# One batch's value loads ahead of GpSimd's gate, and two batches' strided scores one and two tiles later

## The chip, the cores and the metric

The kernel runs on one core of one Trainium2 chip. A core has TensorE (PE in the profile: matmuls; PEld are its weight loads), VectorE (DVE), ScalarE (ACT), GpSimd (POOL) and SyncE (SP), and 16 DMA engines that serve the transfers which these engines issue. The metric is the device time of one execution in microseconds (us). The kernel before was run three times: 310.98, 311.5 and 312.55 us, median 311.5 us. The profile is of one more execution.

## The reference

Windowed attention, then a two-layer network, in float32. Eight batches, eight heads, 576 positions, head dimension 64:

```python
scores = scale * np.matmul(q, k.transpose(0, 1, 3, 2))
rel = pos[:, None] - pos[None, :]
mask_plain = (rel >= 0) & (rel < window)                                   # window = 32
mask_dil = (rel >= 0) & (rel < window * dilation) & (rel % dilation == 0)  # dilation = 4
masks = np.stack([mask_plain if h < H // 2 else mask_dil for h in range(H)], axis=0)
scores = np.where(masks[None], scores, -1e9)
attn = softmax(scores)             # with 1e-9 added to the sum
attn_out = np.matmul(attn, v)
x = attn_out.transpose(0, 2, 1, 3).reshape(B * S, H * D)   # 4608 tokens of 512
h = x @ w_in                                               # 512 x 2048
out = (h * sigmoid(h)) @ w_out                             # 2048 x 512
```

Heads 0 to 3 are "plain" (each query sees the 32 positions up to its own), heads 4 to 7 are "strided" (32 positions in steps of 4).

## The kernel before, in words

**Two kinds of work in one stream.** The order of all instructions is written out by hand. The frame is the network: for each batch b, `layer1(b, f)` (lines 712 to 727) makes 16 tiles of the first layer, f = 0 to 15. A tile is 8 matmuls into `h`, and ScalarE's Silu from `h` into `gT`. `layer2` (lines 769 to 791) then makes four output tiles `o` for an even batch and five for an odd one, each of 16 matmuls in four groups of four, which VectorE copies and SyncE stores. Between the tiles stands the attention of the batches that follow. `plan_of(b)` (lines 811 to 929) is a timetable: `at(s, fn, ...)` puts a call at step s of batch b, and `plan(s)` makes the calls of step s in the order in which they were put there. Steps 0 to 15 stand ahead of the tiles f = 0 to 15, step 16 ahead of the first group of layer 2, step 17 ahead of the second group, and so on.

**Attention of one batch.** z = 0 means the plain heads and z = 1 the strided ones.
- `load_qk` or `load_rows` (123 to 144) bring queries and keys into one of two `nat` buffers. GpSimd issues them, and they convert float32 to float16 on the way. `load_rows(b)` of batch 3 and 4 starts with a memset.
- From batch 3 on, `cross(b, z)` (146 to 159) has SyncE issue DMA transposes into `plain` (L152, two of them) or `strided` (L158, L159). Batch 1 and 2 use TensorE for it (`transpose`).
- `scores(b, z)` (491 to 531): 64 small matmuls into `s` and 16 (strided) or 8 (plain) into `ss`, at L391 or L379; then VectorE's masking and maxima (L512, L521, L528). `shift` (L538) subtracts the maxima, for one half of the heads.
- `exps`, `normal`: exponentials on ScalarE, sums and normalization on VectorE; `turn_by_dma` transposes the result by a DMA that SyncE issues.
- `load_v(b)` (173 to 193) brings the values into `vw`, of which there are two, used in turn: two transfers of L177, two of L185, one of L190, all issued by GpSimd. Part of the values is wanted a second time at other partitions: `shift_plain`, `shift_class` (L205) and `shift_over` (L210) copy it, on VectorE or, as `shift_v`, by DMAs that SyncE issues.
- `values(b, z)` (604 to 631): 64 matmuls into `x` (L627) and 8 or 16 into `xs` (L691), which `finish` copies to `xT`, the first layer's input.

**What stands around the change.** During batch 1, step 2 has SyncE issue the shifts of batch 2's values and the transposes of batch 3 (`cross(3, 0)` and `cross(3, 1)`). Step 17 gives GpSimd, in this order: a copy of one column of `plain` into a tile called `latch` (line 876; the profile files it under L927, where the timetable makes its calls), which can run only when the plain transposes of batch 3 have landed and so holds back everything that GpSimd issues after it; then `load_v(3)`; then `load_rows(4)`. Step 21 has the plain scores of batch 3, step 28 the transposes of batch 4. During batch 2, step 0 gives GpSimd `load_v(4)` and `load_rows(5)`; step 6 has the plain values of batch 3, step 11 its strided scores with `shift`, step 12 `cross(5, 0)`, `shift_class(3)` and `shift_over(3)`, step 17 the plain scores of batch 4. During batch 3, step 11 has the strided scores of batch 4, and so on to the end.

Each engine works off its instructions in order, and SyncE and GpSimd also issue their DMAs in order. A DMA issued by GpSimd is of the profile's queue q0 (software), one by SyncE of q1 (hardware). Queues named "instruction" carry program code.

Of the kernel before, what the change touches and what calls it, by code (L numbers as in the profile page):

```python
# [29 lines left out]
def kernel(  # L30
# [764 lines left out]
    def transposes(at, b, z, step):  # L795
        for which in (1, 0):
            at(step, transpose, b, z, which, both)

    def later(at, b, z, steps, copies=(nc.vector.tensor_copy, nc.vector.tensor_copy)):

        for hi in (0, 1):
            if steps[hi] is not None:
                at(steps[hi], normal, b, z, hi)
        for hi in (0, 1):
            at(steps[2], turn, b, z, hi)
        for hi in (0, 1):
            at(steps[2], turned, b, z, hi, copies[hi])
        at(steps[3], values, b, z)
        at(steps[3], finish, b, z, copies)

    def plan_of(b):
        ev = {}

        def at(s, fn, *args):
            ev.setdefault(s, []).append((fn, args))

        def all_exps(b, z):
            for hi in (0, 1):
                at(16, exps, b, z, hi)

        if b == 0:

            at(-16, normal, 0, 1, 1)
            at(-15, shift_class, 0, dve, 1, 2)
            at(-14, normal, 0, 0, 1)
            at(-8, turn, 0, 1, 1)
            at(-8, turned, 0, 1, 1, act)
            at(-4, turn, 0, 0, 1)
            at(-4, turned, 0, 0, 1)
            at(-4, values0, 1, 1)  # L830
            at(-4, last_values, 0, 1, (1,))
            at(-4, finish0, 1, 1)
            at(-4, last_finish, 0, 1, 1)
            at(-2, values0, 0, 1)
            at(-2, last_values, 0, 0, (1,))
            at(-2, finish0, 0, 1, both)
            at(-2, last_finish, 0, 0, 1)
            at(-2, clear_short, 1, nc.vector)
            at(-2, load_v, 1)
            for c in (2, 3):  # L840
                at(-2, load_w_out, c)
            at(-2, load_qk, 2)
            transposes(at, 1, 1, 2)
            at(8, scores, 1, 1)
            for hi in (0, 1):
                at(8, shift, 1, 1, hi)
            for which in (1, 0):
                at(17, transpose, 1, 0, which, (dve, dve))
            at(20, normal, 1, 1, 0)
            at(20, scores, 1, 0)  # L850
            at(14, shift_v, 1, nc.sync.dma_start)
            at(17, load_rows, 3)
            at(17, load_v, 2)
            all_exps(1, 1)
            for hi in (0, 1):
                at(20, exps, 1, 0, hi)
            for n, z, hi in ((20, 1, 1), (26, 0, 0), (28, 0, 1)):
                at(n, normal, 1, z, hi)
            for n, z, copies in ((27, 1, (dve, dve)), (30, 0, both)):
                for hi in (0, 1):  # L860
                    at(n, turn, 1, z, hi)
                for hi in (0, 1):
                    at(n, turned, 1, z, hi, copies[hi])
                at(n + 1 + z, values, 1, z)
                at(n + 1 + z, finish, 1, z, both)
        elif b == 1:
            transposes(at, 2, 0, 2)
            transposes(at, 2, 1, 11)
            at(2, shift_v, 2, nc.sync.dma_start)
            for z in (0, 1):  # L870
                at(2, cross, 3, z)
                at(28, cross, 4, z)
            at(8, scores, 2, 0)
            for hi in (0, 1):
                at(8, shift, 2, 0, hi)
            at(17, nc.gpsimd.tensor_copy, latch, qTs[1][:, 1, S - 1 : S])
            at(17, load_v, 3)
            at(17, load_rows, 4)
            at(14, scores, 2, 1)
            all_exps(2, 0)  # L880
            all_exps(2, 1)
            for hi in (0, 1):
                at(19, normal, 2, 0, hi)
            at(21, scores, 3, 0)
            at(21, exps, 3, 0, 0)
            at(21, exps, 3, 0, 1)
            later(at, 2, 0, (None, None, 27, 28))
            later(at, 2, 1, (29, 31, 33, 34))
        else:
            if b + 2 < B:  # L890
                at(0, load_v, b + 2)
                if b + 3 < B:
                    at(0, load_rows, b + 3, (1, 0))
                if b + 3 < B:
                    at(12, cross, b + 3, 0)
                if b > 2:
                    at(12, cross, b + 2, 1)
            if b + 1 < B:
                at(1 if b == 2 else 0, shift_plain, b + 1, dve, 0, NM)
                at(12, shift_class, b + 1, dve, 0, 2)  # L900
                at(12, shift_over, b + 1, dve)
                if b == 2:
                    later(at, 3, 0, (0, 0, 4, 6))
                else:
                    at(6, values, b + 1, 0)
                    at(6, finish, b + 1, 0)
                at(11, scores, b + 1, 1)
                at(11, shift, b + 1, 1, 1)
                all_exps(b + 1, 1)
            if b + 2 < B:  # L910
                at(17, scores, b + 2, 0)
                for hi in (0, 1):
                    at(18, exps, b + 2, 0, hi)
            if b + 1 < B:
                for hi in (0, 1):
                    at(22 + hi, normal, b + 1, 1, hi)
                    at(22 + hi, turn_by_dma, b + 1, 1, hi)
                at(29, values, b + 1, 1)
                at(29, finish, b + 1, 1)
            if b + 2 < B:  # L920
                for hi in (0, 1):
                    at(27 + hi, normal, b + 2, 0, hi)
                    at(27 + hi, turn_by_dma, b + 2, 0, hi)

        def plan(s):
            for fn, args in ev.pop(s, ()):
                fn(*args)  # L927

        return plan
# [49 lines left out]
    for b in range(B):  # L979
        plan = plan_of(b)  # L980
        if b == 0:
            for x in range(NFF):
                plan(2 * x - NFF)
                plan(2 * x + 1 - NFF)
                layer1_part(2 * x % NFF, 2 * x // NFF, first[x] if x < 4 else None)
        else:
            for f in range(NFF):
                plan(f)
                layer1(b, f)
        if b == 0:  # L990
            layer2_first(plan)
        else:
            layer2(b, plan)
        for s in range(NFF, 3 * NFF):
            plan(s)
# [30 lines left out]
```

## Time and profile before

| what | value |
|---|---|
| median of three runs | 311.5 us (310.98 to 312.55) |
| the profiled execution, whole | 311.39 us |
| its span, first to last instruction | 309.5 us |
| PE busy | 297.5 us (96%), 4466 matmuls |
| weight loads (PEld) | 191.0 us (62%) |
| ScalarE, VectorE, GpSimd busy | 186.3, 180.0, 91.9 us |
| chain that ended last | PE 82%, DMA 7%, VectorE 5%, ScalarE 2%, issue 2% |
| TensorE's granted clock | 1.00 |

How to read it: the chain of work is followed back from the last instruction, at each step to what released it or to the instruction before it on its engine. A piece called "issue" is time in which an engine waited for nothing that the profile shows. In the timeline's rows come start, length, engine, line, operation, tiles (out<-in) and, in brackets, the idle time before with what ended it. In rows of DMA queues come packets, megabytes, and the packets' own time as a share of 16 engines; packets overlap, so it can go over 100%. Windows are in us from the span's start.

### The profile page before, as it was taken

How to read it: one execution, taken by the hardware profiler on the slowest of the kernel's cores; microseconds unless marked ns; L12 is line 12 of the kernel's file. 1: busy time of each engine (PE TensorE's matmuls, PEld its weight loads, DVE VectorE, ACT ScalarE, POOL GpSimd, SP SyncE). 2: the span in 40 equal slices, each digit the busy share in tenths (PEclk: the TensorE clock that was granted, in tenths of full speed). 3: DMA queues.
4: the chain of work that ended last, by engine and by line, in shares of the span. 5: the costliest groups of instructions: out<-in, count | busy, mean ns of one | idle time of the engine just before them, and what ended most of it. 6: DMA issues, size and time to landing. Idle time of an engine off the chain costs nothing.

```text
span 309.5 us, 10365 instructions
## 1 busy us (share of the span) xinstructions
PE 297.5 (96%) x4466; PEld 191.0 (62%) x4466; DVE 180.0 (58%) x372; ACT 186.3 (60%) x554; POOL 91.9 (30%) x139
## 2 busy tenths in 40 slices
PE   5889999999999979999999999999999999999995
PEld 2657754677555866467644786467744775467544
DVE  6896589627797728852796238862795244620011
ACT  1776667766993548946594458945694558336300
POOL 8544545920693721096005730040000000000000
PEclk9999999999999999999999999999999999999999
DMA  8999999998999999599988998498027000410022
GB/s 107 175 213 200 174 200 215 185 186 125 156 183 172 164 195 110 145 169 150 112 130 162 187 123 130 109 153 123 2 58 162 34 4 0 137 44 2 1 100 70
DMA packets 104878, 39.21 MB, mean 127 GB/s; under 512 B 79568, under 2 KB 100048, under 8 KB 104832
## 3 DMA queue, kind: packets, MB, share of 16 engines
q0 software_dynamic: 63104, 18.88, 62.1%
q1 hardware_dynamic: 41584, 19.60, 30.6%
q8 instruction: 35, 0.57, 0.8%
q14 instruction: 11, 0.09, 0.1%
q10 hardware_dynamic: 144, 0.07, 0.1%
HBM read 37.75 MB, written 9.44 MB: 152 GB/s over the span
## 4 chain that ended last, share of the span: by engine, by line
PE 82%; DMA 7%; DVE 5%; ACT 2%; issue 2%; POOL 1%; POOLq 0%; SPq 0%; ACTq 0%
PE h L717 35%; PE o L782 29%; PE o L756 5%; DMA w_in<-in_moe_w_in_dram 4%; PE h L737 4%; PE x L627 3%; DMA nat<-in_q_dram 2%; PE s L391 1%; PE s L379 1%; ACT pe L560 1%; DVE pn L576 1%; PE t L329 1%; DMA ptT<-pn 1%; DVE ms L512 1%; PE pt L585 1%
## 5 line engine op out<-in xcount | busy, mean ns | idle before, releaser
L725 ACT ACTIVATE gT<-h 128x576 f16<-128x576 f32 x112 | 72.8, 650 | 80.8 <-PE h L717 80.7
L782 PE MATMUL o<-w_out,gT 128*128 128x512 f16 (+1 forms) x528 | 114.2, 373 | 0.0
L717 PE MATMUL h<-xT,w_in 128*128 128x288 f16 x896 | 113.5, 286 | 0.0
L717 PEld LDWEIGHTS <-w_in 128*128 128x128 f16 x896 | 86.4, 98 | 23.3 <-DVE xT L704 0.3
L782 PEld LDWEIGHTS <-gT 128*128 128x128 f16 x528 | 50.6, 98 | 55.1 <-issue 0.2
L560 ACT ACTIVATE pe<-ms,nm 128x64 f32<-128x64 f32 x178 | 59.0, 333 | 4.2 <-DVE nm L528 4.2
L766 DVE COPY ob<-o 128x512 f32<-128x512 f32 (+1 forms) x34 | 23.1, 681 | 46.5 <-PE o L782 45.5
L512 DVE SCALAR_TENSOR_TENSOR ms<-s,mask 128x512 f32<-128x512 f32 x28 | 19.2, 686 | 38.1 <-PE s L391 27.0
L560 ACT ACTIVATION_READ_ACCUMULATOR pe<-ms,nm 128x1 f32 x178 | 33.2, 186 | 0.0
L704 DVE CAST xT<-x 128x512 f16<-128x512 f32 x26 | 16.8, 685 | 21.3 <-PE xs L691 21.3
L177 POOL DMA_DIRECT2D vw<-in_v_dram x16 | 10.0, 636 | 59.0 <-PE xs L691 58.6
L576 DVE TENSOR_TENSOR pn<-pe,r 128x640 f16<-128x640 f32 (+2 forms) x32 | 25.3, 792 | 1.1
L528 DVE TENSOR_REDUCE nm<-ms 128x10 f32<-128x640 f32 (+1 forms) x28 | 22.0, 787 | 1.0
L737 PE MATMUL h<-xT,w_in 128*128 128x256 f16 (+1 forms) x128 | 17.1, 287 | 1.4 <-issue 1.1
L134 POOL DMA_DIRECT2D nat<-in_k_dram x20 | 15.1, 775 | 6.3 <-DMA vw<-in_v_dram 5.5
L134 POOL DMA_DIRECT2D nat<-in_q_dram x20 | 14.6, 756 | 7.6 <-DMA nat<-in_k_dram 5.3
L737 PEld LDWEIGHTS <-w_in 128*128 128x128 f16 x128 | 11.9, 98 | 5.3 <-issue 1.7
L756 PE MATMUL o<-w_out,gT 128*128 128x512 f16 x64 | 15.0, 380 | 0.0
L744 ACT ACTIVATE gT<-h 128x512 f16<-128x512 f32 (+1 forms) x16 | 10.2, 650 | 6.5 <-PE h L737 6.3
L627 PEld LDWEIGHTS <-vw 64*64 64x64 f16 x896 | 8.5, 108 | 5.4 <-issue 5.2
L766 ACT COPY ob_last<-o 128x128 f32<-128x128 f32 x1 | 0.3, 265 | 17.0 <-DVE ob_last L766 17.0
L569 DVE TENSOR_REDUCE l<-pe 128x10 f32<-128x640 f32 (+2 forms) x12 | 9.6, 801 | 1.5 <-ACT pe L551 1.4
(101 smaller groups left out, 262.9 us busy)
## 6 DMA issues: line engine op xcount, KB each, us to landing
out_dram<-ob SPq DMA_DIRECT2D x35, 256.0 KB, 2.5
vw<-in_v_dram POOLq DMA_DIRECT2D x8, 288.0 KB, 7.2
vw<-in_v_dram POOLq DMA_DIRECT2D x16, 128.0 KB, 5.4
w_in<-in_moe_w_in_dram POOLq DMA_DIRECT2D x4, 512.0 KB, 13.3
w_out<-in_moe_w_out_dram POOLq DMA_DIRECT2D x4, 512.0 KB, 11.3
nat<-in_k_dram POOLq DMA_DIRECT2D x6, 256.0 KB, 7.8
nat<-in_q_dram POOLq DMA_DIRECT2D x6, 256.0 KB, 8.2
nat<-in_k_dram POOLq DMA_DIRECT2D x20, 72.0 KB, 7.1
```

The lines of the kernel that those rows point to most:

```text
L134: nc.gpsimd.dma_start(out=f[:, 2 * (1 - which) + h // 2, 0 : ZR - 1, h % 2], in_=src[b, h].rearrange("(m p) d -> p m d", p=RT),)
L512: nc.vector.scalar_tensor_tensor(out=ms[:, 0:8].rearrange("p (n t) c -> p n (t c)", n=2), in0=s[hi].rearrange("p n t c -> p n (t c)"), sca ...
L528: nc.vector.tensor_reduce(out=nm[:, 0:w], in_=ms[:, 0:w], axis=AX.X, op=ALU.max, negate=True)
L560: nc.scalar.activation(pe[:, t, :], slot(t), AF.Exp, scale=1.0 if b else scale, bias=nm[:, t : t + 1], accum_out=l[:, t : t + 1],)
L576: nc.vector.tensor_tensor(pn[:, 0:w], a["pe", z, hi][:, 0:w], r[:, 0:w, None].broadcast_to([P, w, KB]), ALU.mult)
L627: nc.tensor.matmul(dst, w, p, start=True, stop=True)
L717: nc.tensor.matmul(h[:, half, 0:HS], w_in16[:, c, f * P : f * P + P], xT[:, c, half * HS : half * HS + HS], start=(c == 0), stop=(c == MC ...
L725: nc.scalar.activation(gT[:, f, s0 : s0 + S].rearrange("p (a c) -> p a c", a=2), h[:, :, 0:HS], AF.Silu)
L737: nc.tensor.matmul(h[:, i, 0 : c1 - c0], w_in16[:, c, (f + i) * P : (f + i + 1) * P], xT[:, c, c0:c1], start=(c == 0), stop=(c == MC - 1),)
L756: nc.tensor.matmul(o, gT[:, f, t * P : (t + 1) * P], w_out16[:, f, :], start=(f == 0), stop=(f == NFF - 1),)
L766: copy(ob, o)
L782: nc.tensor.matmul(o, gT[:, f, t * P : (t + 1) * P], w_out16[:, f, m0:m1], start=(f == 0), stop=(f == NFF - 1),)
```

## The change

`load_v(3)` is put ahead of the latch at step 17 of batch 1. During batch 2 the strided scores of batch 3, and the `shift` that goes with them, move from step 11 to step 13. During batch 3 those of batch 4 move from step 11 to step 12. All other batches keep step 11. No instruction is added or taken away. Since `shift_class` and `shift_over` stand at step 12 and are put there first, they come ahead of the masking of these scores on VectorE in both batches, where they came behind it before. On GpSimd the five transfers of `load_v(3)` pass the latch. SyncE's order stays as it was.

```diff
@@ -873,8 +873,8 @@
             at(8, scores, 2, 0)
             for hi in (0, 1):
                 at(8, shift, 2, 0, hi)
+            at(17, load_v, 3)
             at(17, nc.gpsimd.tensor_copy, latch, qTs[1][:, 1, S - 1 : S])
-            at(17, load_v, 3)
             at(17, load_rows, 4)
             at(14, scores, 2, 1)
             all_exps(2, 0)
@@ -904,8 +904,9 @@
                 else:
                     at(6, values, b + 1, 0)
                     at(6, finish, b + 1, 0)
-                at(11, scores, b + 1, 1)
-                at(11, shift, b + 1, 1, 1)
+                x = {2: 13, 3: 12}.get(b, 11)
+                at(x, scores, b + 1, 1)
+                at(x, shift, b + 1, 1, 1)
                 all_exps(b + 1, 1)
             if b + 2 < B:
                 at(17, scores, b + 2, 0)
```

## The prediction

> **What bounds the kernel now.** I read the page first, then the busy time by stretches, then the chain of work that ended last, then the DMA queues in narrow windows. The page, its part 1 and its row for the queue that carries program code:
>
> ```profile
> span 309.5 us, 10365 instructions
> ...
> PE 297.5 (96%) x4466; PEld 191.0 (62%) x4466; DVE 180.0 (58%) x372; ACT 186.3 (60%) x554; POOL 91.9 (30%) x139
> ...
> q8 instruction: 35, 0.57, 0.8%
> ```
>
> TensorE (PE) is busy in 297.5 of 309.5 us and the next engine in 186.3, so only TensorE's idle time is worth anything. Four stretches of the view by stages: the one before the steps that change, and three that hold the same work, the first layer of batch 2, 3 and 4. The columns after the stretch are its length and the busy time of PE, PEld, VectorE, ScalarE and GpSimd; the last three are granted clock, DMA share and GB/s:
>
> ```profile
> 59.00:99.50 40.50, 40.45 (x726) 25.92 (x726) 27.59 (x54) 30.22 (x101) 19.27 (x30) 1.00 1.37 166
> 99.50:119.20 19.70, 17.95 (x290) 14.20 (x289) 11.51 (x24) 9.75 (x15) 10.42 (x14) 1.00 1.89 167
> 134.80:152.90 18.10, 17.46 (x281) 13.72 (x280) 9.10 (x16) 9.75 (x15) 9.54 (x13) 1.00 1.48 143
> 172.00:189.30 17.30, 17.30 (x281) 13.64 (x280) 8.72 (x16) 9.75 (x15) 6.20 (x9) 1.00 1.39 149
> ```
>
> TensorE idles 0.05 us in the first stretch, 19.70 - 17.95 = 1.75 us in batch 2's first layer, 0.64 us in batch 3's and nothing in batch 4's; the idle time falls with the DMA share (1.89, 1.48, 1.39). The chain of work shows the place:
>
> ```profile
> 75.42 0.72 PE s L391 x60
> ...
> 105.87 0.61 PE x L627 x64
> 106.48 0.06 PE xs L691 x8
> 106.54 5.01 PE h L717 x40
> 111.55 0.51 PE s L391 x52
> 112.06 1.75 issue
> 113.81 0.27 PE s L391 x12
> ...
> 119.20 0.86 PE o L782 x4
> 120.06 0.70 PE s L379 x64
> ...
> 140.68 0.61 PE x L627 x64
> 141.36 5.01 PE h L717 x40
> 146.36 0.61 PE s L391 x64
> 147.01 0.64 issue
> 147.65 0.27 PE ss L391 x12
> ```
>
> Both stops lie inside the strided scores (L391) of the next batch, and end with "issue": nothing that the profile records was waited for. The first comes after 52 of the 80 matmuls of that step, the second after 68 (80 less the 12 that follow); neither place begins a new tile. What the two have in common is their distance in the program. Here are TensorE's counts from the first stop to the second (view by stages), and the code queue in the same stretch (DMA view of 112 to 147.6):
>
> ```profile
> 112.06:147.64 35.58, 33.20 (x513) 21.43 (x511) 21.32 (x42) 23.16 (x76) 15.43 (x22) 1.00 1.29 151
> q8 instruction: 4, 0.07, 0.7%
> ```
>
> About 512 matmuls with as many weight loads, 1024 instructions, and four code packets: one packet of 0.57 MB / 35 = 16 KB for each 256 instructions, and 35 x 256 = 8960 is the 2 x 4466 of part 1. So I read the stops as TensorE reaching the end of a block of 128 pairs whose successor has not arrived. Each packet's start and length come from the DMA view of windows in which it starts: 69.3 to 69.4, 110.8 to 111.0, 116.4 to 116.5, 145.0 to 145.1 and 148.8 to 149.0 (the share times 16 engines times the window is the packet's length):
>
> ```profile
> q8 instruction: 1, 0.02, 77.0%
> q8 instruction: 1, 0.02, 52.7%
> q8 instruction: 1, 0.02, 77.2%
> q8 instruction: 1, 0.02, 66.9%
> q8 instruction: 1, 0.02, 38.1%
> ```
>
> They last 1.23, 1.69, 1.24, 1.07 and 1.22 us. The second ends at about 112.5 and TensorE goes on at 113.81, 1.3 us later; the fourth ends at 146.1 and TensorE goes on at 147.65, 1.5 us later. Both packets fit the stops. When was each asked for? If it is at the block boundary before, 128 pairs back from 112.06: 52 scores, 40 first-layer matmuls and 8 of xs leave 28 of the 64 of L627, so 106.2. The fetch took 106.2 to 113.8 = 7.6 us, 4.6 of them before the packet started. For the second stop (4 + 64 + 40 + 8 leave 12) it is 141.2 to 147.65 = 6.5 us. A block whose 128 pairs run in less than that stops TensorE.
>
> **The change part by part: scores of batch 3 two tiles later.** A first-layer tile is 8 matmuls, 5.01 / 5 = 1.00 us. No instruction is added, so the block boundary stays at the same place of the program. 16 first-layer pairs now stand ahead of it and 16 of the scores' pairs behind it; a score pair takes 0.51 / 52 = 9.8 ns. TensorE reaches the boundary at 112.06 + 2.00 - 0.16 = 113.90, and the block was ready at 113.81: the stop of 1.75 us goes, with 0.1 us to spare. What is late next is the following block. It now holds 44 score pairs (0.43), three tiles (3.01), the four of layer 2 (0.86) and 56 pairs of the plain scores L379 (0.70 / 64 x 56 = 0.61): 4.9 us, where before it had 6.5. If its packet comes as in the row of 116.4 (113.81 to 116.4 + 1.24 + 1.3 to 1.5 = 119.0 to 119.2, 5.2 to 5.4 us), TensorE stops 0.3 to 0.5 us inside the plain scores; if as in the row of 148.8 (1.2 + 1.22 + 1.3 to 1.5 = 3.7 to 3.9 us after 147.65), not at all. I take 0.2, since the DMA queues should be emptier there than before (below).
>
> On VectorE the masking of these scores moves behind the two shifts of values (L205, L210), which before ended the stage:
>
> ```profile
> 118.38 0.68 DVE L205 COPY vw<-vw 32x2048 f16<-32x2048 f16 x1
> ```
>
> The shifts now run in VectorE's idle time at tile 12 (11.51 busy of 19.70), and the masking starts when the scores end, at 111.55 + 2.00 + 80 x 0.0098 = 114.3, where the scores ended at 113.81 + 28 x 0.0098 = 114.1 before. I cost this at nothing; without the idle time it would be the 0.68 us and L210's smaller copy, once.
>
> **Scores of batch 4 one tile later.** TensorE reaches the boundary at 147.01 + 1.00 - 0.08 = 147.93; ready at 147.65. The stop of 0.64 us goes with 0.28 to spare. The next block holds 20 score pairs (0.20), four tiles (4.01), the 0.86 and all 72 plain scores (0.79): 5.9 us against the 3.7 to 3.9 above, so no new stop. VectorE's order changes in the same way, at no cost.
>
> **Batch 3's values ahead of the gate.** GpSimd's own rows (start, length):
>
> ```profile
> 79.51 0.19 POOL L927 COPY latch<-plain 128x1 f16<-128x1 f16 x1 [14.54 <-DMA plain<-nat]
> 80.12 1.23 POOL L177 DMA_DIRECT2D vw<-in_v_dram  x2 [0.43 <-issue]
> 84.07 2.98 POOL L134 DMA_DIRECT2D nat<-in_k_dram  x4
> 97.56 1.23 POOL L177 DMA_DIRECT2D vw<-in_v_dram  x2 [5.03 <-PE xs L691]
> ```
>
> The five transfers of load_v(3) were issued from 80.12 to before 84.07 and now go from 65.0 (79.51 - 14.54) to about 70, in the 14.5 us that GpSimd stood at the gate. Their target was last read by batch 1's values, long before. Behind the gate, batch 4's rows (a memset and 12 transfers, the first at 84.07) come up to 4 us earlier, less what the gate opens later. Batch 4's values at 97.56 wait for TensorE and stay. So rows and transposes of batch 4 clear the queues earlier, which is where the fetch of 106.2 to 113.8 lost its time. The price is in front of the gate. SyncE's transposes of batch 3, the same transposes under load (DMA view of 72 to 77, then of 91 to 96: kB and median us to landing), the moved transfers' own time (view of 80 to 84), and the reader on TensorE:
>
> ```profile
> 72.48 3.89 SPq L152 DMA_TRANSPOSE plain<-nat  x2
> plain<-nat SPq DMA_TRANSPOSE x2, 5.5
> plain<-nat SPq DMA_TRANSPOSE x2, 9.4
> vw<-in_v_dram POOLq DMA_DIRECT2D x2, 128.0 KB, 4.5
> 82.56 0.68 PE L379 MATMUL s<-plain 64*32 64x64 f16 x64
> ```
>
> The plain transposes opened the gate at 79.5 and batch 3's plain scores read them at 82.56: 3.0 us of cover. From 9.4 - 5.5 a crowded queue would add 3.9 us, and no delay is the other end. The moved values, issued by 70 and 4.5 us on their way, are gone by about 75, so they overlap the first 2.5 us of the 7 us between issue and gate: I take +1.5 us, which the cover hides. The four small copies of shift_v(2) ahead of them on SyncE are not waited for by its queue. The code packet of 69.3 (ready at about 69.3 + 1.23 + 1.5 = 72.0) is wanted in the strided scores of batch 2, at 75.4 or after (the boundary five blocks of 128 pairs ahead of the first stop); with the longest wait seen, 4.6 us against the shortest, 1.2, it would be ready at 75.4, and with that one's longer packet at 75.9: a stop of at most 0.5. I take none.
>
> **Sum.** Against the profiled execution, 311.39 us with its span of 309.5: 311.39 - 1.75 - 0.64 + 0.2 = 309.2; the median of the runs, 311.5, stands 0.1 higher, and I leave another 0.1 for the two narrow margins: 309.4, or -0.7%. No more than 2.4 us can be gained, since TensorE has no other idle time near these steps. The three runs spread over 310.98 to 312.55, so about 0.5% (1.56 us) is what can be told from no change.
>
> [...]
>
> **The rivals.**
> 1. *The wait comes back elsewhere*: late code in the shortened block (0.5), in the strided scores of batch 2 near 75.4 (0.5), or again at the first boundary, whose margin is 0.1, where each 1 us of later packet costs 0.9. For: every margin is below 0.5 us and the packets' delays vary from 1.2 to 4.6. Against: the load on the queues falls at 98 to 113. 0.5 to 1.9 us come back: 309.9 to 311.3, say 310.6.
> 2. *The change does not do what it says*: the stops belong to the scores themselves and move with them. For: both stand in L391. Against: batch 4's stretch has the same scores and no stop, and the places 52 and 68 differ. No gain: 311.4.
> 3. *Slower: the transposes before the gate are late*. If the values crowd out SyncE's transposes, scores of batch 3 wait at 82.56. It costs from a delay of 3.0 us, and outweighs the gain from 3.0 + 2.4 = 5.4. With 3.9 us on the landing of each and SyncE's issue of 3.89 us twice as long, 7.8 us: a stop of 4.8, so 309.2 + 4.8 = 314.0. Against: the crowd is gone by about 75.
>
> **How the numbers follow.** Forecast 0.60 (309.0 to 309.9), the first rival 0.22, the second 0.07, the third 0.11, of which 0.08 beyond +0.5% and 0.03 within. Faster by over 0.5%, under 309.94, is the forecast alone: 0.60. Within 0.5%: 0.22 + 0.07 + 0.03 = 0.32. Slower: 0.08. The range runs from 308.8 (nothing given back, less 0.3 for the runs' spread) to 311.7, the top of the first two rivals with that spread, leaving out the third and a little below: some 0.15.
>
> **What would show it.** In the changed profile: no "issue" piece in L391 in either stretch, at most 0.5 us in L379 near 119; load_v(3) issued from about 65 with the gate after it; L152's landing and the gate at about 80 to 81.5; no TensorE idle time before L379 at 82.6; busy equal to length in the stretches of batch 3. It would be wrong if a stop stands in L391 or L379, or TensorE waits on plain<-nat near 82.6.

## The result and the profile after

The changed kernel takes 308.18 us (median of four runs, 308.01 to 309.07) against 312.02 for the kernel before in the same comparison: ratio 0.9889, 95% interval 0.985 to 0.9928. A second comparison gave 308.27 against 311.06, ratio 0.9911 (0.9883 to 0.9938). It is faster, by 2.8 to 3.8 us, where 2.1 had been forecast, and 308.18 lies below the stated range. The profiled execution took 308.01 us.

The page of the changed kernel, its span and part 1:

```profile
span 306.2 us, 10365 instructions
...
PE 296.8 (97%) x4466; PEld 190.8 (62%) x4466; DVE 179.6 (59%) x372; ACT 186.2 (61%) x554; POOL 92.3 (30%) x139
```

The same three stretches, the first layers of batch 2, 3 and 4, in the view by stages:

```profile
98.84:116.64 17.80, 17.80 (x290) 14.16 (x289) 10.74 (x23) 9.75 (x15) 10.50 (x14) 1.00 1.71 172
132.27:149.57 17.30, 17.30 (x281) 13.66 (x280) 8.96 (x16) 9.77 (x15) 9.91 (x13) 1.00 1.59 148
168.55:185.85 17.30, 17.30 (x281) 13.66 (x280) 8.70 (x16) 9.76 (x15) 6.21 (x9) 1.00 1.45 163
```

The columns are those of the view by stages in the prediction. TensorE now has no idle time in any of them. The DMA share is 1.71 and 1.59, hardly under the 1.89 of before and over the 1.48, so the queues are still crowded. The chain of work after, over the places of the two stops:

```profile
98.82 3.92 PE h L717 x32
...
105.89 6.97 PE h L717 x56
112.85 0.61 PE s L391 x64
113.46 0.14 PE ss L391 x16
...
132.25 5.88 PE h L717 x48
...
144.80 0.61 PE s L391 x64
145.41 0.13 PE ss L391 x16
...
168.53 5.88 PE h L717 x48
```

Seven tiles (x56) now stand ahead of the 64 + 16 strided scores of batch 3, which run through, as those of batch 4 do. The rows of the chain of before at the same three places:

```profile
99.48 3.92 PE h L717 x32
...
134.80 5.88 PE h L717 x48
...
171.96 5.88 PE h L717 x48
```

From first layer to first layer, batch 2's stage took 134.80 - 99.48 = 35.32 us and takes 33.43; batch 3's took 37.16 and takes 36.28. That is 1.89 and 0.88, together 2.77 us of the 3.3 by which the spans differ. Another 0.66 lies ahead of 99 us; what follows batch 3's stage is 0.13 longer than before. In the two stages 1.75 + 0.64 us is the idle time that is gone; most of the remaining 0.4 is score matmuls that take less time when they run through (below).

### The profile page after: what moved, and what is told of

It reads as the page before. It is cut to its first block, busy times and chain, and to the rows that moved or that the text cites. A ratio compares the mean times of both kernels' runs of the same rounds, so it can differ in the third digit from the quotient of the medians.

```text
span 306.2 us, 10365 instructions
## 1 busy us (share of the span) xinstructions
PE 296.8 (97%) x4466; PEld 190.8 (62%) x4466; DVE 179.6 (59%) x372; ACT 186.2 (61%) x554; POOL 92.3 (30%) x139
## 4 chain that ended last, share of the span: by engine, by line
PE 92%; DVE 2%; ACT 2%; issue 1%; DMA 1%; POOL 1%; POOLq 0%; SPq 0%
PE h L717 36%; PE o L782 33%; PE h L737 5%; PE o L756 5%; PE x L627 3%; PE s L391 2%; PE s L379 2%; PE pt L585 1%; ACT pe L560 1%; PE t L329 1%; DMA ptT<-pn 1%; PE t L369 1%; PE xs L691 1%; DVE pn L576 1%; PE s L444 1%
## 5 line engine op out<-in xcount | busy, mean ns | idle before, releaser
L766 DVE COPY ob<-o 128x512 f32<-128x512 f32 (+1 forms) x34 | 23.1, 680 | 46.5 <-PE o L782 45.4
L134 POOL DMA_DIRECT2D nat<-in_k_dram x20 | 15.1, 764 | 5.4 <-DMA vw<-in_v_dram 4.5
L627 PEld LDWEIGHTS <-vw 64*64 64x64 f16 x896 | 8.6, 108 | 5.4 <-issue 5.2
```

What stands on the lines that cost most here:

```text
L134: nc.gpsimd.dma_start(out=f[:, 2 * (1 - which) + h // 2, 0 : ZR - 1, h % 2], in_=src[b, h].rearrange("(m p) d -> p m d", p=RT),)
L627: nc.tensor.matmul(dst, w, p, start=True, stop=True)
L766: copy(ob, o)
```

## The experiments

**Is it the scores or the block of code?** In this kernel 24 tiny matmuls stand ahead of batch 2's first tile and nothing is moved:

```diff
+        for _ in range(24 if (b, f) == (2, 0) else 0):
+            nc.tensor.matmul(h[0:QB, 0, 0:KB], ident[0:D, 0:QB], ident[0:D, 0:KB], start=True, stop=True)
         for c in range(MC):
```

> The kernel before with 24 tiny matmuls (32x64) added in front of batch 2's first tile, written to a place that this tile overwrites; nothing else is moved. Late code: the boundaries move by 24 pairs against the scores, so the stops stand after 28 instead of 52 strided score matmuls in batch 3's and after 44 instead of 68 in batch 4's, with the same operands and about the same length (0.9 to 2 us, 0.2 to 0.7). If the stops belong to the scores: after 52 and 68 as before.

Its chain of work at the two places:

```profile
112.77 0.31 PE s L391 x28
113.08 1.78 issue
114.86 0.44 PE s L391 x36
...
149.19 0.45 PE s L391 x44
149.63 0.65 issue
150.28 0.33 PE s L391 x20
```

The stops stand after 28 and 44 matmuls, to the matmul where they were expected, and last 1.78 and 0.65 us as before (1.75, 0.64). They belong to a place in the program counted in instructions, not to the scores. Its one time was 314.08 us, and the profile tells why. The 24 matmuls took 0.80 us, 33 ns each, and right behind the first stop the granted clock fell to 0.50 for some 3 us: the five first-layer tiles there took 6.68 us instead of 5.01. The row of the view by stages, with a mean clock of 0.74:

```profile
115.44:122.12 6.68, 6.68 (x42) 4.67 (x42) 5.17 (x9) 2.60 (x4) 2.28 (x4) 0.74 1.60 124
```

**Each part alone.** First the values' move without the scores' move:

```diff
+            at(17, load_v, 3)
             at(17, nc.gpsimd.tensor_copy, latch, qTs[1][:, 1, S - 1 : S])
-            at(17, load_v, 3)
```

> Only load_v(3) ahead of the gate; the scores stay at step 11. Late code: the boundary stays inside the strided scores of batch 3 at pair 52, its block runs 5.9 us; the fetch that took 7.6 us should shorten to about 6.6 as it did with the whole change, so a stop of 0.5 to 1.0 us is left there, and the 0.64 us stop of batch 4 stays: 1.0 us faster than before (0.5 to 1.8). If the stops belong to the scores and the values' place has nothing to do with them: same as before, within 0.3 us. If the moved values are what gained the most of the 3.8 us: 2 us or more.

310.52 us against 311.58, ratio 0.9953 (0.9924 to 0.9983). Its chain of work:

```profile
110.77 0.51 PE s L391 x52
111.28 0.89 issue
...
145.27 0.44 issue
```

The first stop is at the same matmul and shorter than the 1.75 and 1.25 us in two profiles of the kernel before (the second is below). The second, 0.44 us, lies between their 0.64 and 0.22, so nothing is shown there. Then the scores' move without the values' move, twice:

```diff
+                x = {2: 13, 3: 12}.get(b, 11)
-                at(11, scores, b + 1, 1)
-                at(11, shift, b + 1, 1, 1)
+                at(x, scores, b + 1, 1)
+                at(x, shift, b + 1, 1, 1)
```

> Only the scores' move (two tiles, one tile); load_v(3) stays behind the gate. Late code: both stops in the strided scores go (2.4 us and about 0.15 us of refill each), the shortened block after the first boundary runs 4.8 us against a fetch of 5.2, so 0.0 to 0.5 us come back in the plain scores of batch 4: 2.0 to 2.7 us faster. If the stops belong to the scores: they move with them and nothing is gained. If the values' move is needed for the gain: under 1 us.

> Only the scores' move, once more. Its first profile had a stop of 2.5 us in the plain scores of batch 4 at 118.9, inside the block that the move shortens to 4.8 us. Late code: again no stop in L391, and one of 0.3 to 2.5 us at the same matmul (after about 56 pairs of L379) or none, by run; runs between 308.4 and 313. If that stop was an accident of that run and not of the block: none there, and other places instead.

309.79 us against 311.58, ratio 0.9947 (0.991 to 0.9983), in twelve runs from 308.41 to 313.58; the second time 312.08 against 311.06, ratio 0.9994 (0.9941 to 1.0046). The chain of work of the first and of the second:

```profile
118.35 0.55 PE s L379 x56
118.89 2.50 issue
```

```profile
118.31 0.55 PE s L379 x56
118.86 2.07 issue
```

Both stops in L391 are gone, and one of more than 2 us has come up one block later, after exactly the 56 plain score pairs that the prediction had counted. In these two profiles moving the scores alone moves the wait. It need not do so each time: both profiles are of longer runs (312.26 and 312.49 us), and five of the sixteen runs took 309.0 us or less, as the changed kernel does. With both parts all ten runs stay within 308.0 to 309.3. The packet of that next block, DMA view of 119.1 to 119.2 in the first of the two:

```profile
q8 instruction: 1, 0.02, 54.9%
```

It ends at about 120.0, 6.0 us after the boundary ahead of it (36 matmuls into L391, at 114.0), and at 119.65, 5.6 us after, in scores_again. In the two profiles of the changed kernel the same packet ends 2.4 and 2.0 us after. So with the values ahead of the gate the next block comes in time.

**What makes the code late.** Four kernels leave work of batch 4 or 5 out of the kernel before.

```diff
-                if b + 3 < B:                       # no_rows5
+                if b + 3 < B and b != 2:
                     at(0, load_rows, b + 3, (1, 0))
-                at(0, load_v, b + 2)                # no_v4; no_loads has both
+                if b != 2:
+                    at(0, load_v, b + 2)
-                at(28, cross, 4, z)                 # no_strided4
+                if z == 0:
+                    at(28, cross, 4, z)
```

> The kernel before without load_rows(5): the queries and keys of batch 5 are not loaded, so its output is that of stale rows, and 12 transfers fewer are on the queues between 101 and 121. Late code because of crowded queues: the first stop (after 52 matmuls, 1.75 us) goes or shrinks below 0.4, the fetch near 106 to 113 takes under 6 us instead of 7.6; the second stop, whose queues are as before, stays at 0.2 to 0.7. If the fetch is late whatever is on the queues: the first stop stays above 0.9.

> The kernel before without load_v(4) alone (batch 4's values are stale; load_rows(5) stays). If the values, sharing the DMA engines with batch 4's strided transposes, make the fetch late: no first stop, or under 0.4 us, since load_rows(5) alone did not matter when it was the one left out. If any of GpSimd's loads beside the transposes is enough: the first stop stays above 0.9 us.

> The kernel before without the strided transposes of batch 4 (cross(4, 1)): that batch's strided scores are of stale operands. The first stop (1.75 us after 52 score matmuls) survived when load_rows(5) was left out. If the fetch of 106 to 113 is late because these transposes and batch 4's values share the DMA engines: the first stop goes or shrinks under 0.6 us, and the second stays. If GpSimd's loads alone delay it: it stays above 0.9 us.

> The kernel before without load_v(4) and load_rows(5): batch 4's values and batch 5's queries and keys are stale. GpSimd has nothing on the queues from about 99 to 131, and SyncE's transposes of batch 4 run alone. If crowding is needed at all: no first stop, fetch under 5 us. If the fetch takes over 7 us in any company, or the transposes alone delay it: it stays above 0.9 us.

For each, in this order, the row of the chain where the first stop stood, and its code packet from the DMA view of a window of 0.1 us (starting at 111.1, 111.5, 110.1 and 107.4):

```profile
112.31 1.77 issue
q8 instruction: 1, 0.02, 99.5%
```

```profile
112.51 1.48 issue
q8 instruction: 1, 0.02, 60.1%
```

```profile
112.34 0.13 issue
q8 instruction: 1, 0.02, 60.9%
```

```profile
111.22 0.61 PE s L391 x64
q8 instruction: 1, 0.02, 67.6%
```

Without batch 5's rows or without batch 4's values the stop is within the 1.25 to 1.75 us of the kernel before, without both there is none, and without batch 4's strided transposes there is almost none. So my reason that the rows crowd the queue, and then that the values do, both fell: in these profiles, one of each, it takes SyncE's strided transposes together with either of GpSimd's two loads. With the loads gone the packet ends at about 108.5, 2.6 us after its block boundary (36 of the 64 matmuls of L627, in that run at 105.9); in the kernel before it ended 6.3 us after. In no_loads the second stop went too. Their single times, 311.72, 311.54, 310.07 and 308.30 us, fit: the last is the changed kernel's.

**Other shifts of the blocks.** Two kernels move the boundaries by tiny matmuls, as above, to find out whether that alone helps: 64 ahead of everything on TensorE, and 80 at the place of the 24.

> The kernel before with 64 tiny matmuls (32x64, about 10 ns each) added at the start of TensorE's stream, where it waits for its first data; nothing else is moved. They shift every block boundary by 64 pairs. Late code: the boundary that stood at pair 52 of the strided scores of batch 3 now stands 12 pairs ahead of them, inside a first-layer tile, and its block runs 7.1 us instead of 5.9; the first stop shrinks to 0 to 0.8 us and shows in L717 near 110, a second of up to 1.0 us may show 128 pairs on, in the first layer near 116; the boundary that stood at pair 68 in batch 4 now stands at pair 4 and its stop shrinks to nothing. 0.6 to 2.4 us faster. If the stops belong to the scores: both stay in L391 after 52 and 68 matmuls, and the time is 0 to 0.7 us longer.

> The kernel before with 80 tiny matmuls ahead of batch 2's first tile (about 0.8 us of TensorE's time), nothing else moved. Late code: the boundaries now stand 28 pairs ahead of batch 3's strided scores and 12 ahead of batch 4's, both inside first-layer tiles, in blocks of about 7 us; no stop in L391, at most 1 us in a first-layer tile near 109 to 116. 1.0 to 2.0 us faster than before in spite of the added work. If the stops belong to the scores: 0.8 us slower, both stops in L391.

Both are slower: 316.02 us, ratio 1.0106 (1.0055 to 1.0156), and 313.40, ratio 1.005 (1.0017 to 1.0084). In neither profile is there a stop in L391, as expected. But the boundaries come down elsewhere. The chain of work of pad64, at its start and in the values of batch 1, and of shift80, in a first-layer tile of batch 2:

```profile
5.25 3.52 PE busy L935 x64
...
20.92 1.49 issue
...
64.17 2.44 issue
```

```profile
99.77 2.43 PE h L716 x80
...
103.90 1.61 issue
```

I had looked only at the blocks near the scores. The pads also cost more than the 10 ns each that I had assumed: 55 ns in pad64 and 30 in shift80, so 3.52 and 2.43 us instead of 0.6 and 0.8. With the stop of 1.49 us that is about the 5 us by which pad64 is late at 33 us. In pad64's profile, the longest of its runs (319.92 us), the granted clock is 0.50 from 66 to 72 us, right behind the stop of 2.44: two first-layer tiles, 16 matmuls, took 3.84 us there, and 1.99 in the kernel before.

The new stops too stand whole blocks apart, counted in matmuls by the view by stages: 256 and 512 in pad64 (from the stop at 20.92 to one at 36.98, and on to 64.17), twice 128 in shift80 (from 103.90 to smaller ones at 112.72 and 119.97). The second row of pad64:

```profile
36.98:64.17 27.19, 26.24 (x512) 15.60 (x512) 20.95 (x39) 17.41 (x54) 18.83 (x30) 1.00 1.31 160
```

**The kernel before and the changed kernel once more.**

> The kernel before, profiled and timed once more, for how much its stops vary from run to run. Late code: stops again after 52 and 68 matmuls of the two strided scores, since the boundaries are fixed in the program, but of another length (1 to 3 us together 2 to 4), because the queues differ by run. Time the same, ratio 1 within 0.3%. If its typical run stops longer than the profiled one, that is the 1.1 us by which the change gained more than the two traces show.

> The changed kernel once more, profiled and timed in more runs. Late code: no stop in L391, at most 0.5 us in L379 near 118; first layers of batch 2 and 3 with what follows as short as in the first profile of it (33.4 and 36.3 us), and what differs between its runs lies ahead of 99 us. Ratio to the kernel before 0.989 to 0.992. If the first four runs of it were lucky: 0.994.

The kernel before: 311.44 us, ratio 0.9998 (0.997 to 1.0026). Its chain of work:

```profile
66.68 0.41 PE s L379 x40
67.09 1.23 issue
...
111.89 0.51 PE s L391 x52
112.40 1.25 issue
```

The stop in L391 is at the same matmul with another length, and there is one at 67.1 that the first profile had not. From that stop to the one at 112.4 the view by stages counts 768 matmuls, six blocks. The changed kernel's second profile (308.27 us in the median, as told above) has none from 42 us to the end of batch 3's stage.

**A better version?** Both profiles of the changed kernel still stop at 41 us for 0.4 to 0.5 us, in batch 1's plain transposes. Two kernels lengthen that block and the one of 67.1:

```diff
-                at(17, transpose, 1, 0, which, (dve, dve))
+                at(18, transpose, 1, 0, which, (dve, dve))
-            at(17, load_rows, 3)                    # best2 alone
-            at(17, load_v, 2)
+            at(18, load_rows, 3)
+            at(18, load_v, 2)
-            at(8, scores, 2, 0)
+            at(9, scores, 2, 0)
             for hi in (0, 1):
-                at(8, shift, 2, 0, hi)
+                at(9, shift, 2, 0, hi)
```

> The changed kernel with two more steps moved by the same reading: the plain scores of batch 2 (and their shift) during batch 1 from step 8 to 9, where one profile of the kernel before stopped for 1.2 us at 67.1, and the plain transposes of batch 1 from step 17 to 18 of batch 0, where both profiles of the changed kernel stop for 0.4 to 0.5 us at 41.3. Late code: no stop at 41 or 67; 0.3 to 0.6 us faster than the changed kernel, ratio to the kernel before about 0.990. If the stop only moves on to the next block: as the changed kernel.

> The changed kernel with two blocks ahead of 99 us lengthened: batch 2's plain scores and their shift from step 8 to 9 of batch 1, and batch 1's plain transposes from step 17 to 18 of batch 0 together with load_rows(3) and load_v(2), which overwrite what they read (best1 moved the transposes alone and so read the rows of batch 3 after waiting for them: 15.9 us at 42.0). If the early stops are late code too: none at 41 or 67, 0.3 to 0.6 us faster than the changed kernel, ratio to the kernel before about 0.990 and a narrower spread. If they only move on: as the changed kernel, 308.2; if the later rows and values of batch 3 and 2 cost more than that: slower than it.

best1 took 332.18 us, a mistake of mine: the transposes stood behind `load_rows(3)`, which reuses their buffer, so they waited for batch 3's rows and batch 1's plain scores were of those rows. best2 took 308.79 us, ratio 0.9908 (0.9871 to 0.9945), the changed kernel's time. The stop at 41 is gone; it stood three blocks (384 matmuls) behind one at 21.1, so it fits late code. Of the stop at 67 best2 says nothing, since neither profile of the changed kernel had it. The plain scores now wait 0.35 us for VectorE at 45.4. Nothing beat the changed kernel. The stop at 21 to 22 us, 0.41 to 1.10 us long in both profiles of both kernels, was left alone.

## Why the prediction was right or wrong

**Right: what the stops are.** Late code in blocks of 128 pairs, the reading on which the sum rested, is supported by shift24 (24 matmuls added, both stops 24 matmuls earlier), by no_loads (the packet ends 2.6 us after its boundary, and there is no stop) and by the counts between stops (128, 256, 384, 512 and 768 matmuls). The second rival, that the stops belong to the scores, is out. When a packet is asked for no trace shows: that it is at the boundary before was my estimate. Of the 35 packets of a profile few go with a stop: TensorE's waits that end with "issue" are 1.10, 1.75 and 0.64 us in the first profile of the kernel before, and 0.85 and 0.37 us in that of the changed kernel. In the runs above the stops at such places lasted from 0.13 us (no_strided4) to 2.50 (scores_only).

**Right: both stops go; the first margin was wider than forecast.** The code packets of the changed kernel, DMA view of 109.6 to 109.8 and of 114.6 to 114.7:

```profile
q8 instruction: 1, 0.02, 29.5%
q8 instruction: 1, 0.02, 57.4%
```

The first ends at about 110.6, usable by 112.1 with the 1.3 to 1.5 us of before, about 1 us ahead of the boundary (after 36 matmuls from 112.85, so 113.2). A margin of 0.1 had been forecast, with the packet as late as before.

**Wrong: the sum.** It had 1.75 + 0.64 less 0.2 less 0.1, and the 2.4 us of the two stops as the most that can be gained; the range's floor allowed 0.3 below that. This step failed. The two stages alone gained 2.77 us, and 0.66 us more lies ahead of them. Three terms were mis-sized:
1. A stop was taken at the length of its "issue" piece. The stages show 1.89 and 0.88 instead of 1.75 and 0.64: 0.4 us more. The score matmuls around a stop are longer too: 0.51 + 0.27 + 0.12 = 0.90 us around the first, against 0.61 + 0.14 = 0.75 when they run through.
2. I gave 0.2 us back in the shortened block and 0.1 for the margins. Nothing came back: the second packet ends at 115.5, usable by about 117.0, and is wanted 56 pairs into L379, at 118.1. For the scores' move alone, though, the 0.3 to 0.5 us that I took as the most, and the first rival's price of 0.5, were far too low: there it came 2 us and more too late. The mechanism was right.
3. The floor of the range allowed 0.3 us for the runs' spread. The profiled run of before took 311.39 us and its median in this comparison was 312.02. Runs of that kernel spread over 310 to 314 us and more, while the changed kernel's stay within 308.0 to 309.3. The traces show two sources: stops in other blocks (67.1 us in one profile) and the start (batch 1's first layer begins at 59.2 and 57.9 us in two profiles of the kernel before). Whether the granted clock is a third is not shown: five runs of the kernel before at a mean of 0.995 took 312.4 to 313.6 us, and six at 0.983 took 310.2 to 312.4. Nor is it shown how much each source adds.

The 2.77 us of the two stages from the profiled 311.39 give 308.6, inside the range; the rest to 308.0 is the 0.66 us ahead of 99 us. The edit touches nothing ahead of 65 us, where the chains differ by 0.4 to 0.5 us, so that much is luck. The remaining 0.2 us lies between batch 2's strided scores, at 75 us, and the end of its first values (L627), at 90 to 91. This stretch is 15.1 to 15.3 us in the five profiles with the values' move and 15.2 to 15.7 in the eleven without, so some of it may be the move's; that stays open.

**Right: the values ahead of the gate, and why it pays.** GpSimd's and SyncE's rows after:

```profile
65.26 0.63 POOL L177 DMA_DIRECT2D vw<-in_v_dram  x1
...
80.77 0.19 POOL L928 COPY latch<-plain 128x1 f16<-128x1 f16 x1 [10.46 <-DMA plain<-nat]
...
81.35 2.94 POOL L134 DMA_DIRECT2D nat<-in_k_dram  x4
...
72.48 6.11 SPq L152 DMA_TRANSPOSE plain<-nat  x2
...
97.75 3.72 SPq L158 DMA_TRANSPOSE strided<-nat  x1
```

The values go at 65.3 (forecast 65.0), the gate opens at 80.8 (80 to 81.5), 1.3 us later than before; the plain transposes of batch 3 are issued in 6.11 us instead of 3.89, and TensorE does not wait for them. So the slower rival's delay was real, 1.3 us, inside its cover of 3. Batch 4's rows go 2.7 us earlier. The prediction had the rows and transposes of batch 4 clear the queues earlier; it did not single out the strided transposes. They start earlier and so run less against batch 4's values and batch 5's rows. SyncE's row for them before, and their median time to landing in the DMA view, before, after and in scores_only:

```profile
99.83 4.70 SPq L158 DMA_TRANSPOSE strided<-nat  x1
```

```profile
strided<-nat SPq DMA_TRANSPOSE x2, 10.3
```

```profile
strided<-nat SPq DMA_TRANSPOSE x2, 8.3
```

```profile
strided<-nat SPq DMA_TRANSPOSE x2, 12.9
```

They start 2.1 us earlier, of which 0.7 is the whole stage's, and land after 8.3 instead of 10.3 us; in scores_only, where they landed after 12.9 us, the next block was 2.5 us late. Other profiles agree: with the values' move they start at 97.5 to 98.2 us (four profiles), without it at 99.3 to 103.1 (seven, of kernels without added matmuls). In no_strided4, without them, 0.13 us of the first stop is left; that the values' move helps through them is argued from these rows, and was not tried by itself.

## What to carry to other kernels

A stop of TensorE that ends with "issue" inside a run of tiny matmuls may be code that has not arrived: count the instructions between two such stops, look for the code queue's packets, and test it by adding a few tiny matmuls ahead, which must bring the stop that many matmuls earlier, as 24 did in shift24. The remedy has two sides, more slow work in the block that is short and fewer transfers in the queues while it is fetched, and the first alone may only hand the wait to the next block, as in the profiles of scores_only and scores_again (2.50 and 2.07 us there). Value such a stop by the stage around it and by several runs: in two profiles of the kernel before the stop at one matmul was 1.75 and 1.25 us long, and one of 1.23 us at 67.1 was in one of them alone.

## What the runs showed of the hardware

A code packet of 16 KB took 0.88 to 1.69 us in the first profile of the kernel before and 0.88 to 1.98 in that of the changed kernel, 35 packets each. For the block of the first stop, it took from block boundary to packet's end 2.6 us with GpSimd's two loads left out (no_loads) and 6.3 us with loads and DMA transposes together (the kernel before). After the packet's end it took TensorE another 1.25 to 1.49 us to go on at the first stop (five profiles: the kernel before, values_only, no_rows5, no_v4, no_strided4), 1.6 at the second in the kernel before, and 1.4 and 1.3 at the stop one block later in scores_only and scores_again. The two stages of the kernel before were 0.14 and 0.24 us longer, against the changed kernel's, than the idle pieces of their stops. In shift24 and pad64 the granted clock fell to 0.50 right behind a stop of 1.78 and 2.44 us. By the mean clocks (0.995 of 312.3 us, 0.989 of 318.1) that would be some 3 and 7 us at 0.50, an estimate that takes the rest at 1.00. In the kernel before, behind a stop of 1.75 us, it stayed at 1.00. What decides this is not shown.
